# First query group of batches 1 to 3: one unsplit fp32 score product, three tiles in one PSUM bank, and another judge of the planned order

## The chip, the cores and the metric

The program runs on one core of one Trainium2 chip. The metric is the device time of one execution in microseconds (us). A core has the engines PE (TensorE, matrix products), ACT (ScalarE), DVE (VectorE), POOL (GpSimd) and SP (SyncE, which here only issues transfers). Products land in PSUM, which has eight banks of 512 fp32 columns on each of 128 partitions.

## The reference: what is computed

Block-causal attention over 4 batches, 8 heads, 576 positions and head size 64, and behind it two feed-forward layers over the 2304 x 512 result:

```python
scores = q @ k.T / sqrt(64)               # masked: 64-wide key blocks up to the query's own
x = softmax(scores) @ v                   # -> 2304 x 512
h = x @ w_in                              # 512 x 2048
y = softplus(h) @ w_out
xn = y / rms(y) * rms_g
out = (silu(xn @ w_gate) * (xn @ w_val)) @ moe2_w_out
```

All of it is held to fp32 accuracy, so most products are written as three products of split operands.

## The kernel before

**Operands and products.** TensorE takes most operands as `F32R`. An fp32 operand is split into a high part (a rounded copy) and a low part (the difference), and a product is three matmuls: high by high, high by low, low by high (`PASSES`). The alternative is one matmul on fp32 operands as they are ("unsplit"), which the trace records as two weight loads and two matmul records, where a split product has three of each.

**Attention.** A unit `u` is (batch b, query group g, head pair p). There are 48: 4 batches, 3 groups of 192 queries, 4 head pairs. A unit has three tiles (`ib` 0 to 2), each of 128 rows (64 queries of two heads) against `n = 64*(3g+ib+1)` keys: 64, 128 and 192 keys in group 0. `s_tile` (from L594) makes a tile's scores with its product (L617 to L619), then takes the row maximum on DVE (L627) and calls `s_exp` (exponential on ACT from the same PSUM bank, L661), `s_norm` (L669, L670) and `s_split` (L681 to L686), after which a transposing transfer (`pt<-pst`, L693) turns the probabilities for the product with V in `pv`. Every score tile has a PSUM bank of its own. `R_a` gives three banks to scores and to the outputs of `pv` once batch 0 is done.

**Batch 0** (`whole(u)`, units 0 to 11) already uses unsplit fp32 scores, straight from the loaded q and k, and scales the maximum with a small operation (L639). **Batches 1 to 3** (36 units) split q and k first: `prep_q` (L533) copies q into the high part (L327 on ACT or L329 on POOL), takes the difference (L337 on DVE or L338 on POOL) into `qbd`, and then issues the load of q for unit u+2 into the freed slot of `qf` (two slots). `prep_k` (L541) makes `khl` from the loaded k (L547 ACT, L552 DVE). The loaded k and v share a ring `R_raw` of three buffers.

**Layer 1** runs beside attention: `g1` (L817, `b<-x,w`) makes h for 384 rows and 128 features, ACT and DVE make softplus into a ring buffer `t` (L833 to L836) and split it into `g` (L327, L337), and `g2` (`b<-g,w`) multiplies by the second matrix. `R_t` is the ring of `t` with four buffers; the squares of `evac_b` (L889) and the gating of layer 2 (L931 to L935) use it too. Layer 2 is `g34` and `g5`, from about 600 us to the end.

**Order.** No engine's order is written out by hand. Every operation is handed to `Plan` with an engine, an assumed duration and a due time (`key`). `Plan.schedule` lays them out in time; `Plan.emit` (L268) repeats this, each time mixing the due times with the latest possible starts of the last layout, and emits all operations by the starts of the best layout. Each engine, and SP's queue too, then runs its list strictly in that order. `schedule` also models TensorE's clock, with a fixed offset of 0.7 us between the plan's time and the clock's windows.

Of the kernel before, what the change touches and what calls it, by code (L numbers as in the profile page):

```python
# [68 lines left out]
class Plan:  # L69
# [72 lines left out]

        return (e == "POOL" and not self.ops[i][6]) or (e == "DVE" and i in self.shared)

    def schedule(self, key):

        n = len(self.ops)
        eng, took = [o[0] for o in self.ops], [o[1] for o in self.ops]
# [40 lines left out]
        for _ in range(n):  # L189
# [24 lines left out]
                port_free = t + dur  # L214
            start[i] = t
            if e == "PE":
                rest, share, dur, z = dur, self.cols[i] / dur, 0.0, t + 0.7
# [53 lines left out]
    def emit(self):  # L271
        n = len(self.ops)
        self.edges()
        key = [o[2] for o in self.ops]
        best = None
        for r in range(12):
            try:
                end, start, ends, bank, choice, eng, took = self.schedule(key)
            except TypeError:
                break  # L280
            if best is None or end < best[0]:
                best = (end, start, bank, choice, key)
# [61 lines left out]
def kernel(  # L344
# [63 lines left out]
    R_x = Ring(com, 2, [128, KD, 2, BLK], F32R, "x")  # L408
    R_y = Ring(com, 1, [128, KD, BLK], FP32, "y")
    R_g = Ring(com, 3, [128, 2, BLK], F32R, "g")  # L410
    R_t = Ring(com, 4, [128, BLK], FP32, "t")
    R_wraw = Ring(com, 2, [128, CW], U64, "wraw")
    R_wa = Ring(com, 2, [128, CW], FP32, "wa")
    R_wA = Ring(wp, NA, [128, 2, 2, CW], F32R, "w")
# [6 lines left out]
    def mm(o, l, r, start, stop):  # L421
        nc.tensor.matmul(o, lhsT=l, rhs=r, start=start, stop=stop)  # L422
# [54 lines left out]
    qf = [kp.tile([128, NG, 128], FP32, name=f"qf{i}") for i in range(NQF)]  # L477
    qbd = [kp.tile([128, 2, NG, 128], F32R, name=f"qbd{i}") for i in range(2)]
    R_raw = Ring(ap_, 3, [128, KT * 128], FP32, "raw")
    R_am = Ring(ap_, 2, [128, 3], FP32, "am")  # L480
    R_P = Ring(ap_, 3, [128, KT * 128], FP32, "P")
    R_nm = Ring(ap_, 2, [128, 16], FP32, "nm")
# [12 lines left out]
    def whole(u):  # L495
        return u < 12

    def load_k(b, p, key):
        t = raw["k", b, p] = R_raw.new()
        att_ops.append(load(key, lambda: t()[:, 0:S], kT[b, p], writes=[t], nbytes=294912))  # L500

    k_y = R_y.new()
    k_raw = [R_raw.new() for p in range(2, NP)]
# [26 lines left out]
        att_ops.append(load(key, lambda: t().rearrange("p (a b) -> p a b", a=KT), vP[b, p], writes=[t], nbytes=327680))  # L530

    def prep_q(u, key):
        if whole(u):  # L533
            return
        t, d = qf[u % 2].rearrange("p i c -> p (i c)"), qbd[u % 2].rearrange("p l i c -> p l (i c)")
        hi, lo = (lambda: d[:, 0]), (lambda: d[:, 1])
        rd = [("qf", u % 2)]
        aop2(copies(nc, 384, hi, lambda: t, ("ACT", "POOL")), key, rd, [("qbd", u % 2, 0)])
        aop2(differences(nc, 384, lo, lambda: t, lambda: hi().bitcast(FP32), ("DVE", "POOL")), key, rd + [("qbd", u % 2, 0)], [("qbd", u % 2, 1)])
        if u + 2 < len(units):  # L540
            load_q(u + 2, key)  # L541
# [41 lines left out]
    def ring_a(u):  # L583
        return R_a0 if u * NG < len(units) * NG // NB else R_a
# [7 lines left out]
    part = {}  # L592

    def s_tile(u, ib, key, after):  # L594
        b, g, p = units[u]
# [10 lines left out]
        if whole(u):  # L606
            kt, k = k_cell(p), lambda: k0(p)
            (qc, qt), kr = q_slot(u), [kt]
            qr = [qc]
        bank = []  # L610
        for c0, cn in chunks:
            sp = ring_a(u).new()
            bank.append(sp)

            def qk(sp=sp, c0=c0, cn=cn):
                if whole(u):
                    mm(sp()[:, :cn], qt()[:, ib, :], k()[:, c0:c0 + cn], True, True)  # L617
                    return
                for m, (a, c) in enumerate(PASSES):  # L619
                    mm(sp()[:, :cn], d[:, a, ib, :], khl[p][:, c, c0:c0 + cn], m == 0, m == 2)  # L620

            if c0 == 0:
                qk_op.append(len(plan.ops))
            aop("PE", max(0.213, 0.006 + cn * 1.667e-3) if whole(u) else 3 * t_mm(cn), key, qk, qr + kr, [sp], after=after, cols=t_mm16((4 if whole(u) else 3) * cn))
        for c, (sp, (c0, cn)) in enumerate(zip(bank, chunks)):
            col = ib + c
            aop("DVE", t_dve(cn), key, lambda sp=sp, col=col, cn=cn: nc.vector.tensor_reduce(nm()[:, col:col + 1], sp()[:, :cn], axis=AX.X, op=ALU.max, negate=True), [sp], [(nm, ib)])  # L627
# [3 lines left out]
        if whole(u):  # L631
            if 0:
                if ib < NG - 1:
                    return
                todo, i0, i1 = done, 0, NG
            else:
                todo, i0, i1 = [done[-1]], ib, ib + 1
# [14 lines left out]

    def s_exp(u, ib, n, bank, chunks, key):
        nm, done = part[u]
        P = part[u, ib] = R_P.new()
        scale = 0.125 if whole(u) else 1.0
        if n % 128:
            aop("POOL", 0.09, key, lambda: nc.gpsimd.memset(P()[:, n:n + 64], 0.0), [], [(P, "pad")])
        for c, (sp, (c0, cn)) in enumerate(zip(bank, chunks)):
            col = 4 + ib + c  # L660
            aop("ACT", 0.24 + cn * 0.836e-3, key, lambda sp=sp, col=col, c0=c0, cn=cn: nc.scalar.activation(P()[:, c0:c0 + cn], sp()[:, :cn], ACTF.Exp, scale=scale, bias=nm()[:, ib:ib + 1], accum_out=nm()[:, col:col + 1]), [sp, (nm, ib)], [P, (nm, "s", ib)])  # L661
# [127 lines left out]
    def attention(t0, t1, when, after):  # L789
        nt = len(tiles)  # L790
        for t in range(t0, t1):
            if t < nt:
# [6 lines left out]
                    load_v(b + 1, p, when(t) - 5)  # L799
                if ib == NG - 1 and b + 1 < B and g == NG - 1 and True:  # L800
                    load_k(b + 1, p, when(t) - 5)
                if ib == NG - 1 and whole(u):
                    if u + 4 < 12 + 2:
                        load_q(u + 4, when(t) - 5)
# [366 lines left out]
```

## Time and profile before

| | before |
|---|---|
| median of 3 runs (lowest to highest) | 1040.03 us (1039.77 to 1041.62) |
| the profiled execution: its own time | 1040.05 us |
| its span, first to last instruction | 1038.3 us |
| PE busy | 1009.9 us (97%) |
| DVE, ACT, POOL busy | 667.8, 580.1, 214.0 us |
| granted TensorE clock, mean | 0.998 |

The profiled execution is thus one of the median's kind, and 1.75 us lie outside of its span. The page's rows count an engine as busy while an instruction runs; a wait row names an instruction that started late, the instruction or transfer that released it, and for how long the engine sat idle before.

### The profile page before, as it was taken

How to read it: one execution, taken by the hardware profiler on the slowest of the kernel's cores; microseconds unless marked ns; L12 is line 12 of the kernel's file. 1: busy time of each engine (PE TensorE's matmuls, PEld its weight loads, DVE VectorE, ACT ScalarE, POOL GpSimd, SP SyncE). 2: the span in 40 equal slices, each digit the busy share in tenths (PEclk: the TensorE clock that was granted, in tenths of full speed). 3: DMA queues.
4: the chain of work that ended last, by engine and by line, in shares of the span. 5: the costliest groups of instructions: out<-in, count | busy, mean ns of one | idle time of the engine just before them, and what ended most of it. 6: DMA issues, size and time to landing. Idle time of an engine off the chain costs nothing.

```text
span 1038.3 us, 16885 instructions
## 1 busy us (share of the span) xinstructions
PE 1009.9 (97%) x6136; PEld 941.9 (91%) x6136; DVE 667.8 (64%) x1592; ACT 580.1 (56%) x1352; POOL 214.0 (21%) x289
## 2 busy tenths in 40 slices
PE   5999899999999999999999999999999999999998
PEld 4677898999989999999999999999999999999997
DVE  6899999887888677777888899422422423222322
ACT  6999798777778678877878664211211212111111
POOL 3543433331233023223324342000000000000000
PEclk9999999999999999999999999999999999999999
DMA  7454787958556635456444634200100100000000
GB/s 263 133 194 150 191 196 167 252 116 201 130 132 117 111 102 183 164 209 212 162 158 159 199 102 142 69 1 1 62 1 1 62 1 1 31 1 1 31 1 31
DMA packets 111635, 115.19 MB, mean 111 GB/s; under 512 B 84544, under 2 KB 92352, under 8 KB 110528
## 3 DMA queue, kind: packets, MB, share of 16 engines
q1 hardware_dynamic: 110976, 107.83, 36.8%
q0 software_dynamic: 576, 6.29, 1.6%
q8 instruction: 48, 0.79, 0.3%
q14 instruction: 35, 0.29, 0.1%
HBM read 72.03 MB, written 21.63 MB: 90 GB/s over the span
## 4 chain that ended last, share of the span: by engine, by line
PE 73%; DVE 9%; ACT 8%; DMA 7%; issue 2%; POOL 1%; SPq 0%; POOLq 0%; ACTq 0%; DVEq 0%
PE b L422 73%; DMA pt<-pst 4%; DMA wraw<-in_w_dram 2%; ACT P L661 1%; POOL wa L461 1%; ACT wa L448 1%; DVE wa L456 1%; DVE g L337 1%; ACT w L327 1%; DVE nm L627 1%; DVE wa L458 1%; DVE pst L686 1%; DVE t L836 1%; ACT t L834 1%; ACT P L705 1%
## 5 line engine op out<-in xcount | busy, mean ns | idle before, releaser
L422 PE MATMUL b<-x,w 128*128 128x384 f32 x2880 | 543.6, 338 | 2.0 <-DVE nm L669 0.8
L422 PEld LDWEIGHTS b<-x,w 128*128 128x128 f32 x2880 | 503.8, 188 | 13.8 <-issue 1.3
L422 PE MATMUL b<-g,w 128*128 128x384 f32 x1152 | 229.8, 339 | 2.2 <-DVE g L337 1.9
L422 PEld LDWEIGHTS b<-g,w 128*128 128x128 f32 x1152 | 199.4, 188 | 6.5 <-DVE g L337 3.6
L422 PE MATMUL b<-w,g 128*128 128x512 f32 x648 | 160.4, 392 | 0.0
L932 DVE TENSOR_TENSOR t<-b,t 128x384 f32<-128x384 f32 x72 | 40.0, 556 | 165.3 <-ACT t L931 165.1
L422 PEld LDWEIGHTS b<-w,g 128*128 128x128 f32 x648 | 120.6, 188 | 21.8
L461 POOL TENSOR_TENSOR wa<-wa,wraw 128x512 int32<-128x512 int32 x68 | 95.2, 1401 | 204.0 <-DVE wa L456 119.1
L931 ACT ACTIVATE t<-b 128x384 f32<-128x384 f32 x72 | 35.2, 490 | 171.8 <-PE b L422 171.8
L934 ACT CAST g<-t 128x384 fp32r<-128x384 f32 x72 | 36.8, 513 | 136.4 <-DVE t L933 136.4
L661 ACT ACTIVATE P<-b,nm 128x288 f32<-128x288 f32 (+8 forms) x160 | 80.1, 502 | 16.3 <-DVE nm L639 4.5
L627 DVE TENSOR_REDUCE nm<-b 128x1 f32<-128x288 f32 (+8 forms) x160 | 70.7, 447 | 18.7 <-PE b L422 17.6
L933 DVE TENSOR_TENSOR t<-b,t 128x384 f32<-128x384 f32 x72 | 39.9, 556 | 61.5 <-PE b L422 61.5
L686 DVE SCALAR_TENSOR_TENSOR pst<-P,nm,pst 128x128 f16<-128x128 f32 (+4 forms) x108 | 68.3, 638 | 9.1 <-ACT pst L683 6.7
L422 PE MATMUL b<-khl,qbd 128*128 128x448 f32 (+7 forms) x360 | 68.9, 312 | 1.0 <-ACT pt L722 1.0
L337 DVE TENSOR_TENSOR g<-t,g 128x384 fp32r<-128x384 f32 x96 | 60.5, 632 | 11.4 <-ACT g L327 10.9
L836 DVE SCALAR_TENSOR_TENSOR t<-b,t 128x384 f32<-128x384 f32 x96 | 52.6, 551 | 21.4 <-ACT t L835 21.0
L935 DVE TENSOR_TENSOR g<-t,g 128x384 fp32r<-128x384 f32 x72 | 42.9, 597 | 35.4 <-ACT g L934 35.4
L422 PEld LDWEIGHTS b<-khl,qbd 128*128 128x128 f32 x360 | 57.1, 188 | 3.9 <-ACT pt L722 1.2
L327 ACT CAST g<-t 128x384 fp32r<-128x384 f32 x96 | 49.2, 516 | 19.9 <-DVE t L836 16.8
L448 ACT ACTIVATE wa<-wraw 128x512 f32<-128x512 f32 x68 | 46.1, 678 | 20.9 <-DMA wraw<-in_w2gv_dram 10.7
L833 ACT ACTIVATE t<-b 128x384 f32<-128x384 f32 x96 | 46.5, 493 | 19.1 <-PE b L422 19.0
(91 smaller groups left out, 1055.7 us busy)
## 6 DMA issues: line engine op xcount, KB each, us to landing
wraw<-in_w_dram SPq DMA_DIRECT2D x32, 512.0 KB, 3.6
wraw<-in_w2gv_dram SPq DMA_DIRECT2D x24, 512.0 KB, 3.6
yd<-y SPq DMA_DIRECT2D x12, 768.0 KB, 3.7
y<-yd SPq DMA_DIRECT2D x12, 768.0 KB, 4.5
qf<-in_qP_dram SPq DMA_DIRECT2D x42, 192.0 KB, 2.8
xd<-x SPq DMA_DIRECT2D x4, 1536.0 KB, 7.1
x<-xd POOLq DMA_DIRECT2D x4, 1536.0 KB, 7.4
wraw<-in_w2o_dram SPq DMA_DIRECT2D x12, 512.0 KB, 4.4
```

The source lines that it names most:

```text
L327: "ACT": ("ACT", t_act(n), lambda: nc.scalar.copy(dst(), src())),
L337: "DVE": ("DVE", t_dve(n), lambda: nc.vector.tensor_tensor(dst(), a(), b(), ALU.subtract)),
L422: nc.tensor.matmul(o, lhsT=l, rhs=r, start=start, stop=stop)
L448: op("ACT", t_act(CW), prio, lambda a=a, hv=halves: nc.scalar.activation(a(), hv()[1].bitcast(FP32), ACTF.Abs), [raw], [a])
L461: op("POOL", t_pool2(CW), prio, lambda a=a, hv=halves: nc.gpsimd.tensor_tensor(a().bitcast(I32), a().bitcast(I32), hv()[0].bitcast(I32), A ...
L627: aop("DVE", t_dve(cn), key, lambda sp=sp, col=col, cn=cn: nc.vector.tensor_reduce(nm()[:, col:col + 1], sp()[:, :cn], axis=AX.X, op=ALU.m ...
L661: aop("ACT", 0.24 + cn * 0.836e-3, key, lambda sp=sp, col=col, c0=c0, cn=cn: nc.scalar.activation(P()[:, c0:c0 + cn], sp()[:, :cn], ACTF.E ...
L686: aop("DVE", t_dve(c, True), key, lambda: nc.vector.scalar_tensor_tensor(lo(), pc(), r(), hi(), ALU.mult, ALU.subtract), [P, (P, "pad"), ( ...
L833: op("ACT", t_act(BLK, False), key - 5, lambda: nc.scalar.activation(e(), h()[:, :BLK], ACTF.Abs), [h], [e])
L836: op("DVE", t_dve(BLK), key - 5, lambda: nc.vector.scalar_tensor_tensor(e(), h()[:, :BLK], 0.0, e(), ALU.max, ALU.add), [h, e], [e])
L932: op("DVE", t_dve(BLK), key + 2, lambda: nc.vector.tensor_tensor(u(), ga()[:, :BLK], u(), ALU.mult), [ga, u], [u])
L935: op("DVE", t_dve(BLK), key + 4, lambda: nc.vector.tensor_tensor(g()[:, 1], u(), g()[:, 0].bitcast(FP32), ALU.subtract), [u, (g, 0)], [(g, ...
```

## The change

1. `unsplit(u)` is `whole(u)` or group 0. The 12 units of group 0 in batches 1 to 3 now make each score tile as one fp32 product of the loaded q and the first 192 columns of the loaded k. These columns get a buffer and a transfer of their own (`R_kg`, two buffers, one 96 KB load per unit, issued behind the load of k). `prep_q` does nothing for these units.
2. Their maximum is scaled by the small operation that batch 0 uses, on DVE or POOL, and the exponential takes the scale 0.125.
3. The three tiles of a group-0 unit go to columns 0, 64 and 192 of one bank; in the plan, each third of the bank is a cell of its own.
4. The load of q for unit u+2 behind a group-0 unit of batches 1 to 3 is issued behind that unit's third tile, not behind its `prep_q`.
5. `R_t` has three buffers instead of four.
6. `emit` makes up to 60 layouts instead of 12 and judges each by its mean end over three clock offsets (0.7, 1.8, 2.9 us). A layout that can't be completed no longer ends the search; its due times are averaged with the best ones.

```diff
+    PHASES = (0.7, 1.8, 2.9)
+    def schedule(self, key, phase=PHASES[0]):
...
-        for r in range(12):
+        for r in range(60):
...
+                mean = (end + sum(self.schedule(key, p)[0] for p in self.PHASES[1:])) / len(self.PHASES)
...
+            if best is None or mean < best[0]:
+                best = (mean, start, bank, choice, key)
...
-    R_t = Ring(com, 4, [128, BLK], FP32, "t")
+    R_t = Ring(com, 3, [128, BLK], FP32, "t")
...
+    R_kg = Ring(ap_, 2, [128, GQ], FP32, "kg")
...
+    def unsplit(u):
+        return whole(u) or units[u][1] == 0
...
+        k = kg[b, p] = R_kg.new()
+        att_ops.append(load(key, k, kT[b, p][:, 0:GQ], writes=[k], nbytes=98304))
...
     def prep_q(u, key):
-        if whole(u):
+        if unsplit(u):
             return
...
+        elif unsplit(u):
+            (qc, qt), k = q_slot(u), kg[b, p]
+            qr, kr = [qc], [k]
         bank = []
+        o0 = (0, 64, 192)[ib] if g == 0 else 0
         for c0, cn in chunks:
-            sp = ring_a(u).new()
+            if g == 0 and ib:
+                sp = packed[u]
+            else:
+                sp = packed[u] = ring_a(u).new()
...
+                if unsplit(u):
+                    mm(sp()[:, o0:o0 + cn], qt()[:, ib, :], k()[:, c0:c0 + cn], True, True)
                     return
...
+                if ib == NG - 1 and unsplit(u) and not whole(u) and u + 2 < len(units):
+                    load_q(u + 2, when(t) - 4)
```

(The packing of item 3 goes by `g == 0`, so the four group-0 units of batch 0 are packed too.)

## Rows read from the trace of the kernel before

**Rows 1.** The page: span, and busy time, share and instructions of each engine.

```profile
span 1038.3 us, 16885 instructions
PE 1009.9 (97%) x6136; PEld 941.9 (91%) x6136; DVE 667.8 (64%) x1592; ACT 580.1 (56%) x1352; POOL 214.0 (21%) x289
```

**Rows 2.** Busy time by stretch: stretch, length, PE, PEld, DVE, ACT, POOL, clock, DMA.

```profile
60.00:140.00 80.00, 73.93 (x512) 64.37 (x511) 75.67 (x227) 71.57 (x181) 34.42 (x51) 1.00 0.61 170
140.00:360.00 220.00, 216.40 (x1711) 202.24 (x1710) 188.48 (x571) 174.41 (x461) 60.13 (x118) 1.00 0.69 155
360.00:600.00 240.00, 238.88 (x1379) 235.02 (x1379) 189.41 (x331) 184.53 (x372) 78.27 (x58) 1.00 0.51 172
```

**Rows 3.** What PE waited for, all of the span: total us, times, longest.

```profile
PE b L422 <- DMA qf<-in_qP_dram: 4.4, 1, 4.4
PE b L422 <- ACT pt L722: 3.0, 4, 1.4
```

**Rows 4.** Chain that ended last, its longest piece: start, us, what.

```profile
582.01 451.67 PE b L422 x2377
```

**Rows 5.** PE in order of time, around a split group-0 unit of batch 3.

```profile
275.82 0.51 PE L422 MATMUL b<-x,w 128*128 128x384 f32 x2
276.17 1.14 PE L422 MATMUL b<-khl,qbd 128*128 128x64 f32 x9
277.15 1.07 PE L422 MATMUL b<-g,w 128*128 128x384 f32 x5
```

**Rows 6.** PE in order of time, unsplit group-0 tiles of batch 0.

```profile
10.05 0.38 PE L422 MATMUL b<-y,pst 128*128 128x64 f32 x2
...
22.50 1.04 PE L422 MATMUL b<-raw,qf 128*128 128x64 f32 x6
...
34.01 0.49 PE L422 MATMUL b<-raw,pst 128*128 128x192 f32 x2
34.20 1.35 PE L422 MATMUL b<-x,w 128*128 128x384 f32 x6
35.39 0.49 PE L716 MATMUL b<-ones,P 128*128 128x128 f32 x3
```

**Rows 7.** PE in order of time, a group-0 tile of batch 1 that waited.

```profile
95.02 0.58 PE L422 MATMUL b<-khl,qbd 128*128 128x192 f32 x3 [1.01 <-ACT pt L722]
```

**Rows 8.** Instructions on `qbd`: duration ns min/median/max, first and last start.

```profile
L338 POOL TENSOR_TENSOR qbd<-qf,qbd x22: 999/1024/1608, 59.8 to 334.9; 128x384 fp32r<-128x384 f32 x22
L327 ACT CAST qbd<-qf x22: 495/510/655, 64.0 to 334.3; 128x384 fp32r<-128x384 f32 x22
L337 DVE TENSOR_TENSOR qbd<-qf,qbd x14: 541/547/860, 99.0 to 313.4; 128x384 fp32r<-128x384 f32 x14
```

**Rows 9.** The scaling of the maximum in batch 0, on DVE, same columns.

```profile
L639 DVE TENSOR_SCALAR nm<-nm x24: 133/143/155, 5.3 to 90.8; 128x1 f32<-128x1 f32 x24
```

**Rows 10.** PE and DVE in order of time: units 0 and 13, scores and maxima.

```profile
4.38 3.75 PE L422 MATMUL b<-y,qf 128*128 128x64 f32 x10 [4.38 <-DMA qf<-in_qP_dram]
5.07 0.23 DVE L627 TENSOR_REDUCE nm<-b 128x1 f32<-128x64 f32 x1 [5.07 <-PE b L422]
...
107.66 0.28 DVE L627 TENSOR_REDUCE nm<-b 128x1 f32<-128x128 f32 x1
107.73 0.47 PE L422 MATMUL b<-khl,qbd 128*128 128x192 f32 x3
```

**Rows 11.** Loads of q, us to landing; PE in order of time, units 14 and 16.

```profile
DMA to landing us min/median/max: 2.3/2.8/6.7
...
114.75 0.38 PE L422 MATMUL b<-khl,qbd 128*128 128x192 f32 x2
...
119.12 0.51 PE L422 MATMUL b<-khl,qbd 128*128 128x256 f32 x3
```

**Rows 12.** ACT and DVE in order of time: a fourth `t` begins.

```profile
255.64 0.49 ACT L833 ACTIVATE t<-b 128x384 f32<-128x384 f32 x1
255.54 0.55 DVE L337 TENSOR_TENSOR g<-t,g 128x384 fp32r<-128x384 f32 x1
```

More of the change, by code (lines that the diff above doesn't have):

```diff
@@ L143, in on_port @@
         return (e == "POOL" and not self.ops[i][6]) or (e == "DVE" and i in self.shared)
-    def schedule(self, key):
+    PHASES = (0.7, 1.8, 2.9)
+    def schedule(self, key, phase=PHASES[0]):
         n = len(self.ops)
@@ L216, in schedule @@
             if e == "PE":
-                rest, share, dur, z = dur, self.cols[i] / dur, 0.0, t + 0.7
+                rest, share, dur, z = dur, self.cols[i] / dur, 0.0, t + phase
                 while rest > 1e-9:
@@ L279, in emit @@
             except TypeError:
-                break
-            if best is None or end < best[0]:
-                best = (end, start, bank, choice, key)
+                if best is None:
+                    raise
+                key = [(x + y) / 2 for x, y in zip(key, best[4])]
+                continue
+            try:
+                mean = (end + sum(self.schedule(key, p)[0] for p in self.PHASES[1:])) / len(self.PHASES)
+            except TypeError:
+                mean = INF
+            if best is None or mean < best[0]:
+                best = (mean, start, bank, choice, key)
             late = self.latest(start, ends, eng, took)
@@ L496, in whole @@
         return u < 12
+    def unsplit(u):
+        return whole(u) or units[u][1] == 0
+    kg = {}
     def load_k(b, p, key):
@@ L590, in small @@
         aop2([e[k] for k in kind], key, reads, writes, False)
-    part = {}
+    part, packed = {}, {}
     def s_tile(u, ib, key, after):
@@ L609, in s_tile @@
             qr = [qc]
+        elif unsplit(u):
+            (qc, qt), k = q_slot(u), kg[b, p]
+            qr, kr = [qc], [k]
         bank = []
+        o0 = (0, 64, 192)[ib] if g == 0 else 0
         for c0, cn in chunks:
-            sp = ring_a(u).new()
+            if g == 0 and ib:
+                sp = packed[u]
+            else:
+                sp = packed[u] = ring_a(u).new()
             bank.append(sp)
             def qk(sp=sp, c0=c0, cn=cn):
-                if whole(u):
-                    mm(sp()[:, :cn], qt()[:, ib, :], k()[:, c0:c0 + cn], True, True)
+                if unsplit(u):
+                    mm(sp()[:, o0:o0 + cn], qt()[:, ib, :], k()[:, c0:c0 + cn], True, True)
                     return
                 for m, (a, c) in enumerate(PASSES):
-                    mm(sp()[:, :cn], d[:, a, ib, :], khl[p][:, c, c0:c0 + cn], m == 0, m == 2)
+                    mm(sp()[:, o0:o0 + cn], d[:, a, ib, :], khl[p][:, c, c0:c0 + cn], m == 0, m == 2)
             if c0 == 0:
                 qk_op.append(len(plan.ops))
-            aop("PE", max(0.213, 0.006 + cn * 1.667e-3) if whole(u) else 3 * t_mm(cn), key, qk, qr + kr, [sp], after=after, cols=t_mm16((4 if whole(u) else 3) * cn))
+            aop("PE", max(0.213 if whole(u) else 0.11, 0.006 + cn * 1.667e-3) if unsplit(u) else 3 * t_mm(cn), key, qk, qr + kr, [(sp, ib)], after=after, cols=t_mm16((4 if unsplit(u) else 3) * cn))
         for c, (sp, (c0, cn)) in enumerate(zip(bank, chunks)):
             col = ib + c
-            aop("DVE", t_dve(cn), key, lambda sp=sp, col=col, cn=cn: nc.vector.tensor_reduce(nm()[:, col:col + 1], sp()[:, :cn], axis=AX.X, op=ALU.max, negate=True), [sp], [(nm, ib)])
+            aop("DVE", t_dve(cn), key, lambda sp=sp, col=col, cn=cn: nc.vector.tensor_reduce(nm()[:, col:col + 1], sp()[:, o0:o0 + cn], axis=AX.X, op=ALU.max, negate=True), [(sp, ib)], [(nm, ib)])
         if len(chunks) == 2:
@@ L630, in s_tile @@
         done.append((ib, n, bank, chunks, key))
[L631 to L637, printed above, removed]
+        if unsplit(u):
+            todo, i0, i1 = [done[-1]], ib, ib + 1
             cells = [(nm, i) for i in range(i0, i1)]
@@ L654, in s_exp @@
         nm, done = part[u]
+        o0 = (0, 64, 192)[ib] if units[u][1] == 0 else 0
         P = part[u, ib] = R_P.new()
-        scale = 0.125 if whole(u) else 1.0
+        scale = 0.125 if unsplit(u) else 1.0
         if n % 128:
@@ L660, in s_exp @@
             col = 4 + ib + c
-            aop("ACT", 0.24 + cn * 0.836e-3, key, lambda sp=sp, col=col, c0=c0, cn=cn: nc.scalar.activation(P()[:, c0:c0 + cn], sp()[:, :cn], ACTF.Exp, scale=scale, bias=nm()[:, ib:ib + 1], accum_out=nm()[:, col:col + 1]), [sp, (nm, ib)], [P, (nm, "s", ib)])
+            aop("ACT", 0.24 + cn * 0.836e-3, key, lambda sp=sp, col=col, c0=c0, cn=cn: nc.scalar.activation(P()[:, c0:c0 + cn], sp()[:, o0:o0 + cn], ACTF.Exp, scale=scale, bias=nm()[:, ib:ib + 1], accum_out=nm()[:, col:col + 1]), [(sp, ib), (nm, ib)], [P, (nm, "s", ib)])
         if len(chunks) == 2:
```

## The prediction

> **What bounds the kernel now.** First the page's busy shares: PE is busy in 1009.9 of 1038.3 us [rows 1], so about 28 us of the span are not PE work, 4.4 of them the first load [rows 3]. Then busy time by stretch, to see where the rest lies: PE lacks 6.1 of 80 us from 60 to 140 us, 3.6 of 220 up to 360, 1.1 of 240 up to 600 [rows 2], together 10.8; another 8 or 9 lie in the first 60 us. In the first of these stretches DVE (75.7 of 80) and ACT (71.6) are as full as PE: there attention is limited by them. From 140 us on PE sets the pace, and from 582 us the chain that ended last is one piece of 451.67 us on PE [rows 4]. So what is taken off PE's list between 140 and 360 us comes off the end one for one, as long as no new wait replaces it; what is taken off DVE or ACT counts only up to 140 us; the clock is at its full level throughout (1.00 in each stretch), so it has nothing to give back.
>
> **The change part by part.** All sums are made against the profiled execution, 1040.05 us (a span of 1038.3 and 1.75 around it), which is 0.02 above the median.
>
> *PE.* A split group-0 unit takes 0.98 us of PE, from its first start at 276.17 to the next product's at 277.15 [rows 5]. That is nine matmuls at about 0.11 us, and the 64-column ones are no cheaper than the 192-column ones: 64, 128 and 192 columns at 2.4 GHz would be 0.03, 0.05 and 0.08 us, so each is held by its own weight load. An unsplit tile has two loads instead of three. Its price from batch 0: a 64-column tile 0.38 us, less the 0.16 by which an end overlaps the next start (276.17 + 1.14 - 277.15 [rows 5]), is 0.22 [rows 6]; a 192-column tile followed by six 384-column matmuls takes 35.39 - 34.01 = 1.38 us, less six times 0.175 (two of them from 275.82 to 276.17 [rows 5]), is 0.33; a 128-column tile lies between, and I take 0.22, since four passes of 128 columns at 2.4 GHz are 0.21. Sum 0.77. The one unit of batch 0 whose three tiles ran in one piece gives 1.04 - 0.16 = 0.88 [rows 6], its first load not hidden. The gain is 0.21 per unit, at worst 0.10: times 12, **-2.5 us** (bounds -1.2 and -2.8). Eight of the twelve units lie behind 140 us, where nothing hides it; of the four before, 0.8 us, a part may turn into idle time, which the bounds take in.
>
> The Trainium skill ("TensorE: Matmul & The Clock Gate", section "Back-to-back issue gap") gives about 81 ns for each pair of a weight load and a 128-column matmul in a sustained stream. By it a split unit would take 0.73 us, an unsplit one about 0.65 by streaming, and the term would be an estimated -1 us; no row here shows a pair below 0.11, so the trace disagrees.
>
> *A wait for a bank.* The third tile of unit 12 waited 1.01 us [rows 7]; its score bank would now be that of its first two tiles. But this is the stretch where DVE and ACT are full. 0 to -1.0; I take half, **-0.5**.
>
> *The shared bank.* In the plan the thirds of a bank are free of each other. If the program keeps engines apart by whole banks, a score product can't run while DVE or ACT reads an earlier third. Of the 24 second and third tiles of batches 1 to 3, seven readings of an earlier tile (maximum or exponential) were running when a tile's product started, as at 107.73, in the midst of the maximum at 107.66 [rows 10]; their remainders add up to 0.7 us. Unit 0 has the same at the very start: its first maximum begins at 5.07 while PE still runs scores [rows 10]; the packing takes batch 0 in too, and there the maximum must wait for one or two products, 0.5 to 1.2 us. I take **+0.7** and **+0.5**; bounds 0 and, together, 2.5 (below nothing only through the banks set free, which the line before has).
>
> *Splitting and scaling.* By their start times, 12 of the 36 preparations of q are of group 0: 5 copies on ACT at 0.51, 3 differences on DVE at 0.55, the other 7 copies and 9 differences on POOL (1.02 each for a difference, up to 1.6) [rows 8]. DVE loses 1.6 us, ACT 2.6, POOL about 15. Scaling adds 36 times 0.143 us if all goes to DVE [rows 9]. In batch 1, where DVE is the limit, that is 12 x 0.143 - 0.55 = +1.2 us at most; ACT's relief and POOL's free time (a third of the scalings of batch 0 went there) speak against it. **+0.3**, bounds -0.5 and +1.2. Behind 140 us PE covers it.
>
> *Queues.* Twelve loads of 96 KB more go through SP, one small issue each; the third of a batch must wait for the first unit's products (two buffers), and the transposing transfers and weight loads queue behind it on SP. Loads of q behind a group-0 unit leave only after its third tile. From unit 14's last product at about 115 us to unit 16's first at 119.12 [rows 11] there are 4.0 us; a load takes 2.8 (up to 6.7), and copy and difference 0.51 + 0.55 to 1.02. This just fits or misses by some us, and then the planned order puts other products first. 0, bounds 0 and +2.
>
> *`t` ring.* With three buffers, one of 96 starts of `t` in layer 1 would have come too early: at 255.64, by 0.45 us, the difference running until 256.09 [rows 12]. Squares of `evac_b` likewise by up to 2 us, but off PE's path. 0.
>
> *The order.* Sixty layouts judged at three offsets find a shorter plan than twelve at one; how much of that is true on the chip no row says. What it can touch is the 19 us in which PE idles up to 600 us without the first load. I take a twentieth, **-1.0**; a new order can as well lose, so -4 and +3.
>
> Sum: -2.5 - 0.5 + 0.7 + 0.5 + 0.3 - 1.0 = -2.5, so **1037.5 us**.
>
> **The rivals.**
> *The bank couples PE to DVE and ACT (slower).* Where the new order sets a unit's second or third product behind the maximum or exponential of the tile before, PE, which runs in order, waits for engines that lag by some us (in unit 13 the first maximum came 3 us behind its product). Without the bank's two terms the sum is -3.7. With unit 0's 0.5, 0.13 us for each of the 24 later tiles eats it up, and from 0.22 on the kernel is slower by 0.2%. At 0.23: 0.5 + 5.5 - 3.7 = +2.3, **1042.3**. For it: the plan knows nothing of it. Against: in 17 of 24 cases nothing overlaps in the order before. The Trainium skill ("PSUM — Partial Sum Buffer", section "PSUM bank collisions raise a hardware error") says just this: two engines on one bank collide even at disjoint columns, so accesses must be guarded by bank, not by address. No run here shows it yet; it is why the rival has a chance of its own.
> *The new order pays.* It takes a fifth of the 19 us: -4 instead of -1, **1034.5**. For it: batch 1 idles most, and 15 us of POOL and a bank or two per unit come free there.
> *The gain is made and eaten elsewhere.* PE's list is 2.5 shorter, but late loads of q (+2) or a fuller DVE (+1.2) and an order no better give it back: **1040**.
>
> **How the numbers follow.** This kernel's measurement can tell about 0.2% from no change, 2.1 us; 1037.97 is the border. Forecast (1036 to 1039.2): 0.45, of it 0.27 faster, 0.18 same. Order pays: 0.20, faster. Eaten: 0.20, 0.18 same and 0.02 slower. Bank: 0.15, 0.12 slower, 0.03 same. So faster 0.47, same 0.39, slower 0.14. The range that leaves out 2 in 10 is 1034.0 to 1042.0; it takes in the bounds of the order's term and most of the bank's.
>
> **What would show it.** Group-0 units with six matmul records and about 0.77 us of PE; PE busy lower by about 2 us and hence its idle time unchanged; no wait as at 95.02. For the bank rival: waits of PE for L627 or L661 in front of group-0 scores, and the first exponential later than 5.52 us. For the third: waits of PE for `qf`, `kg` or L337 at the first units of group 1. The prediction is wrong if PE's idle time up to 600 us changes by more than 3 us either way: then the order, not the product, decided.

## The result, and the profile after

| | before | after |
|---|---|---|
| median of 7 runs (lowest to highest) | 1040.55 us (1039.19 to 1041.62) | 1045.85 us (1043.55 to 1050.10) |
| ratio of the runs, 95% interval | | 1.0055 [1.0037, 1.0072] |
| the profiled execution: time, span | 1040.05, 1038.3 us | 1043.55, 1041.8 us |

The kernel became 5.3 us slower; 1037.5 was forecast, and the range ended at 1042. The profiled execution of after is its fastest run, so its trace shows only 3.5 of the 5.3 us; its mean granted clock is 0.995, and the other six runs had 0.988 to 0.993.

The page of after, span and busy time, answers to [rows 1]:

```profile
span 1041.8 us, 16886 instructions
PE 1011.1 (97%) x6100; PEld 939.8 (90%) x6100; DVE 672.9 (65%) x1608; ACT 567.9 (55%) x1330; POOL 214.4 (21%) x307
```

Busy time by stretch, columns as in [rows 2]; first a row of before that [rows 2] leaves out, then after:

```profile
0.00:60.00 60.00, 47.08 (x263) 34.52 (x264) 47.29 (x170) 49.81 (x143) 25.89 (x53) 0.97 0.64 215
```

```profile
0.00:60.00 60.00, 46.82 (x251) 32.15 (x252) 46.79 (x168) 48.14 (x137) 24.34 (x46) 0.94 0.62 199
60.00:140.00 80.00, 71.73 (x487) 62.20 (x485) 73.57 (x226) 69.89 (x178) 33.56 (x54) 0.98 0.63 185
140.00:360.00 220.00, 214.99 (x1668) 200.25 (x1665) 188.46 (x578) 166.58 (x450) 62.59 (x140) 1.00 0.72 158
360.00:600.00 240.00, 240.00 (x1413) 237.02 (x1412) 192.82 (x334) 179.19 (x365) 74.87 (x56) 1.00 0.49 168
```

PE has 36 instructions fewer than before and is yet busy 1.2 us longer: the clock is lower in the first two stretches (0.94 and 0.98, where before has 0.97 and 1.00). Idle is 30.7 us instead of 28.4. Between 60 and 140 us PE lacks 8.3 us, where it lacked 6.1.

What PE waited for in after (total us, times, longest), to be held against [rows 3]:

```profile
PE b L431 <- DVE x L773: 4.7, 1, 4.7
PE b L431 <- DMA qf<-in_qP_dram: 4.4, 1, 4.4
PE b L736 <- ACT P L725: 3.2, 2, 2.0
PE b L431 <- DMA pt<-pst: 2.7, 2, 1.6
PE b L431 <- DVE nm L651: 2.5, 4, 1.3
```

The 4.4 is the first load, as before. New are one wait of 4.7 us for an `x` (L773) and four for a row maximum (L651).

Engines in order of time at the start of after, four rows picked out (start, duration, engine, line, tiles; in brackets the idle time before and its releaser), to be held against unit 0 in [rows 10]:

```profile
4.38 1.20 PE L431 MATMUL b<-y,qf 128*128 128x64 f32 x4 [4.38 <-DMA qf<-in_qP_dram]
5.61 0.22 DVE L651 TENSOR_REDUCE nm<-b 128x1 f32<-128x64 f32 x1 [5.61 <-PE b L431]
5.89 2.93 PE L431 MATMUL b<-y,qf 128*128 128x192 f32 x6 [0.32 <-DVE nm L651]
7.26 0.31 ACT L681 ACTIVATE P<-b,nm 128x64 f32<-128x64 f32 x1 [5.24 <-DVE nm L651]
```

The first maximum waits for the second product (5.61, before 5.07), the third product waits for that maximum, and the first exponential begins at 7.26 instead of 5.52. So in the running program the thirds of a bank are not free of each other as they are in the plan. These are waits that the program itself makes, for one engine's access to the bank to end before the next begins; what the chip would do without them no run shows.

PE in order of time near 100 us in after:

```profile
100.14 0.93 PE L431 MATMUL b<-kg,qf 128*128 128x64 f32 x6
100.90 0.39 PE L431 MATMUL b<-ones,am 128*128 128x128 f32 x2
...
106.47 3.91 PE L431 MATMUL b<-x,w 128*128 128x384 f32 x12 [4.67 <-DVE x L773]
110.32 1.78 PE L431 MATMUL b<-pt,pst 128*64 128x192 f32 x20
```

An unsplit unit takes 0.76 us (100.14 to 100.90), as forecast. Soon behind it lies the longest pause, and behind that half clock, as two rows by stretch of after show:

```profile
101.80:106.50 4.70, 0.04 (x2) 0.03 (x1) 4.70 (x18) 2.83 (x8) 1.91 (x6) 1.00 0.81 211
106.50:110.20 3.70, 3.70 (x12) 3.42 (x12) 2.77 (x10) 2.87 (x6) 1.86 (x2) 0.54 0.77 211
```

PE did next to nothing for 4.7 us while the granted clock was at the 2.4 GHz level (1.00), and then worked at 1.2 GHz for nearly all of the next 3.7.

### The profile page after: what moved, and what is told of

It is laid out like the page before. It is cut to its first block, busy times and chain, and to the rows that moved or that the text cites. A ratio compares the mean times of both kernels' runs of the same rounds, so it can differ in the third digit from the quotient of the medians.

```text
span 1041.8 us, 16886 instructions
## 1 busy us (share of the span) xinstructions
PE 1011.1 (97%) x6100; PEld 939.8 (90%) x6100; DVE 672.9 (65%) x1608; ACT 567.9 (55%) x1330; POOL 214.4 (21%) x307
## 4 chain that ended last, share of the span: by engine, by line
PE 82%; DVE 8%; DMA 5%; ACT 3%; issue 2%; SPq 1%; POOL 0%; ACTq 0%; DVEq 0%; POOLq 0%
PE b L431 81%; DMA pt<-pst 2%; DMA wraw<-in_w_dram 1%; DVE pst L706 1%; DVE nm L651 1%; DVE w L346 1%; DVE wa L465 1%; PE b L736 1%; ACT P L681 1%; DVE wa L467 0%; DMA qf<-in_qP_dram 0%; DVE g L957 0%; DVE x L937 0%; DVE t L955 0%; SPq L441 0%
## 5 line engine op out<-in xcount | busy, mean ns | idle before, releaser
L651 DVE TENSOR_REDUCE nm<-b 128x1 f32<-128x288 f32 (+8 forms) x160 | 69.8, 450 | 20.1 <-PE b L431 18.5
L706 DVE SCALAR_TENSOR_TENSOR pst<-P,nm,pst 128x384 f16<-128x384 f32 (+4 forms) x108 | 68.7, 649 | 7.7 <-ACT pst L703 4.0
L346 DVE TENSOR_TENSOR g<-t,g 128x384 fp32r<-128x384 f32 x96 | 60.9, 637 | 10.0 <-ACT g L336 9.4
L957 DVE TENSOR_TENSOR g<-t,g 128x384 fp32r<-128x384 f32 x72 | 40.0, 557 | 32.5 <-ACT g L956 32.5
L431 PE MATMUL b<-khl,qbd 128*128 128x448 f32 (+5 forms) x252 | 52.2, 328 | 0.9 <-DVE y L879 0.8
L857 ACT ACTIVATE t<-t 128x384 f32<-128x384 f32 x96 | 50.2, 526 | 1.2
```

The costliest lines, as they stand in the source:

```text
L346: "DVE": ("DVE", t_dve(n), lambda: nc.vector.tensor_tensor(dst(), a(), b(), ALU.subtract)),
L706: aop("DVE", t_dve(c, True), key, lambda: nc.vector.scalar_tensor_tensor(lo(), pc(), r(), hi(), ALU.mult, ALU.subtract), [P, (P, "pad"), ( ...
L857: op("ACT", t_act(BLK), key - 5, lambda: nc.scalar.activation(e(), e(), ACTF.Ln, bias=1.0), [e], [e])
```

## The experiments

"In the old order" and "in the new order" mean that the layout is that of before or of after, instruction by instruction, and only what is named differs. The other kernels lay themselves out. The planned end is what the kernel computes for its layout when it is built, at the single clock offset of 0.7 us. Ratios are to the runs of before on the same chip. Where an expectation speaks of the score tiles of units 0, 1 and 2, it counts the group-0 units of batch 0 alone (0, 2 and 4 among all units).

| run | median us | ratio [95%] | planned end | median less planned |
|---|---|---|---|---|
| before | 1040.55 | 1 | 1021.1 | 19.4 |
| after | 1045.85 | 1.0055 [1.0037, 1.0072] | 1019.8 | 26.0 |
| one_product_only | 1040.20 | 0.9995 [0.9987, 1.0004] | old order | |
| prod_in_old_order | 1055.31 | 1.0150 [1.0134, 1.0165] | old order | |
| pack_unit0_in_old_order | 1040.66 | 1.0006 [0.9995, 1.0017] | old order | |
| new_judge_old_operations | 1045.78 | 1.0048 [1.0035, 1.0061] | 1026.1 | 19.7 |
| old_judge_new_operations | 1040.83 | 1.0003 [0.9994, 1.0011] | 1018.5 | 22.3 |
| other_layout_new_operations | 1045.71 | 1.0054 [1.0041, 1.0068] | 1020.8 | 24.9 |
| old_judge_own_banks | 1043.93 | 1.0034 [1.0022, 1.0047] | 1019.55 | 24.4 |
| old_judge_late_q_planned | 1046.50 | 1.0057 [1.0045, 1.0070] | 1018.44 | 28.1 |
| early_x_in_new_order | 1046.65 | 1.0073 [1.0060, 1.0086] | new order | |
| early_x_of_units_9_10 | 1046.85 | 1.0058 [1.0039, 1.0077] | new order | |
| filled_gaps_in_new_order | 1047.12 | 1.0062 [1.0049, 1.0074] | new order | |
| no_late_q_in_new_order | 1043.99 | 1.0035 [1.0022, 1.0047] | new order | |
| unpack_batch0_in_new_order | 1044.63 | 1.0042 [1.0028, 1.0055] | new order | |
| new_order_own_banks | 1045.84 | 1.0046 [1.0033, 1.0059] | new order | |
| new_order_no_late_q_own_banks | 1040.77 | 1.0006 [0.9995, 1.0016] | new order | |
| old_judge_no_late_q | 1040.81 | 1.0006 [0.9998, 1.0015] | order of old_judge_new_operations | |
| old_judge_own_banks_unit0 | 1041.98 | 1.0016 [1.0005, 1.0026] | the same | |
| filled_gaps_old_judge | 1041.62 | 1.0011 [1.0003, 1.0020] | the same | |

### Does the unsplit product gain anything?

```diff
+                if g == 0:
+                    mm(sp()[:, :cn], d[:, 0, ib, :].bitcast(FP32), khl[p][:, 0, c0:c0 + cn].bitcast(FP32), True, True)
+                    return
```

> The kernel before, its order, banks, copies, differences and loads untouched; only TensorE's three products of each group-0 tile of batches 1 to 3 become one unsplit fp32 product of the two high parts (the low parts of q and k are left out of these scores). By the theory that the unsplit product gains what the prediction said and only the later load of q ate it in the run prod_in_old_order: 2.1 to 2.9 us faster than before, about 1038.2. By the theory that a product saved in a fixed order only turns into idle time: within 0.7 us of before.

The page of one_product_only:

```profile
span 1038.4 us, 16813 instructions
PE 1007.7 (97%) x6100; PEld 938.3 (90%) x6100; DVE 667.2 (64%) x1592; ACT 580.1 (56%) x1352; POOL 214.4 (21%) x289
```

This kernel leaves out the low parts of q and k in these scores. PE works 2.2 us less than before, and the span is the same to 0.1 us: the whole gain lies as idle time on PE. In the stretch of batch 1, from 90 to 160 us, PE waited in before for

```profile
PE b L422 <- DVE g L337: 1.2, 1, 1.2
PE b L422 <- ACT pt L722: 1.0, 1, 1.0
...
PE b L422 <- DMA pt<-pst: 0.5, 1, 0.5
PE b L422 <- ACT P L661: 0.3, 1, 0.3
```

and in one_product_only for

```profile
PE b L422 <- DMA pt<-pst: 1.8, 2, 1.3
PE b L422 <- ACT pt L725: 1.2, 1, 1.2
PE b L422 <- DVE g L337: 1.2, 1, 1.2
...
PE b L422 <- ACT P L664: 0.6, 1, 0.6
```

PE waits longer for the probabilities and their transposing transfers. That this is the gain itself, turned into waits, is likely but not shown: 2.1 of the 2.3 us of additional idle time lie between 60 and 140 us, with only 4 of the 12 units, and the same instructions on DVE and ACT start 0.6 to 2.3 us later than in before between 115 and 290 us, which PE's lighter list does not explain. What the times show is that almost nothing comes off the end: the interval leaves at most 1.4 us of gain.

### What does the later load of q cost, if the order knows nothing of it?

An unsplit product again, but of the loaded q; the splitting of q is gone, and the load leaves later.

```diff
-            load_q(u + 2, key)
+            later[u] = lambda: nc.sync.dma_start(out=tq(), in_=qP[b2, g2_, p2])   # issued behind the unit's third product
```

> The kernel before with its own order of all operations, each score tile in its own bank; only the product of the 12 group-0 units of batches 1 to 3 is one unsplit fp32 product of the loaded q, their splitting of q is gone, and the load of q for the unit after next leaves behind the unit's third product. The keys are the rounded high part of k alone (its low part is left out), so that no further load and no scaling are needed. By the theory that the unsplit product gains what the prediction said: -2.1 to -2.9 us against before, about 1037.8, with about 0.77 us of PE for such a unit instead of 0.98. By the theory that the gain is lost anywhere (late q, or idle time in its place): -1 to +1 us, with PE waiting for qf or idle longer up to 360 us.

It was 15 us slower than before. Waits of prod_in_old_order between 190 and 215 us, one row each of POOL, DVE and PE:

```profile
POOL qbd L362 <- DMA qf<-in_qP_dram: 10.4, 1, 10.4
DVE qbd L370 <- POOL qbd L362: 6.5, 1, 6.5
PE b L455 <- DVE t L922: 6.0, 1, 6.0
```

One late load stops POOL's copy, DVE's difference stands behind it in DVE's list, and layer 1's softplus stands behind that: PE waits 6 us for work that has nothing to do with q. The same instruction on DVE and ACT starts 3.7 us later than in before at 125 us, and 13.7 us later at 220 us. So in an order that does not plan for it the load's place is worth far more than the product; neither of the two theories had foreseen a loss of this size.

### Does the shared bank delay at the start go through?

```diff
+                sx, o0 = shared[u], (0, 64, 192)[ib]      # the first three group-0 units of batch 0
```

> The kernel before with its own order and its split products; only the three score tiles of units 0, 1 and 2 (group 0 of batch 0) share one bank each, at columns 0, 64 and 192. By the theory that the shared bank couples the engines and that the start of the kernel goes straight into its end: the first exponential starts 1 to 1.8 us later than 5.52 us, and the kernel is 1 to 1.8 us slower. By the theory that the delay is taken up later, since PE idles several us up to 140 us: the first exponential is as late, and the time within 0.5 us of before.

The first DVE and ACT work is 1.2 to 1.6 us late, and at 10 us 0.17: the pauses of the old order take it up. The second theory holds, in this order.

### Is it the search or the operations?

```diff
-        for r in range(60):
+        for r in range(12):
...
-                mean = (end + sum(self.schedule(key, p)[0] for p in self.PHASES[1:])) / len(self.PHASES)
+                mean = end
```

> The changed kernel with the old search: 12 layouts, judged at the single clock offset of 0.7 us. It takes another layout (planned end 1018.5 us, where the changed kernel's own is 1019.8 at that offset). By the theory that the new operations cost the time in any order (bank, late q, scaling): the same 23.7 us between plan and chip, hence about 1042.5 to 1045. By the theory that the picked order alone lost, and the old search picks better: 18.9 us between plan and chip as before, hence about 1037.5, at most 1040.

The reverse, the new search with the operations of before:

> The kernel before, all its operations, with the new search alone (60 layouts, judged by their mean end over three clock offsets). It takes another layout than before: mean planned end 1023.1 us where the old one's is 1024.7, but 1026.1 against 1021.1 at the single offset of 0.7 us. By the theory that the search, not the operations, made the loss: slower than before, by 2 to 5 us (1042.5 to 1045.5). By the theory that the operations made it and the mean over offsets judges rightly: 1 to 2 us faster than before, about 1039.

And the sixth layout of the new search (`if r == 5:`):

> The changed kernel with another layout of its own search: the sixth, whose mean planned end (1021.2 us) is 1.1 later than that of the one it takes (1020.06) and 0.8 later than the old judge's (1020.4). It sizes what a layout is worth on the chip beside its planned end. Its longest planned pauses of PE behind 30 us are 2.0 us, where the one taken has 5.7. By the clock theory: clock 0.995 or more and 1040 to 1043. By the theory that the plan ranks layouts rightly: 1 us slower than the changed kernel, 1046 to 1048.

With the old search the changed operations run as fast as before (1040.83, between the ranges of both theories); with the new one the old operations run 5.0 us slower. So the layout that the new search takes makes nearly the whole loss, with either set of operations. Both searches go through the same layouts in the same order as far as the old one goes: of the changed operations the new search takes the eighth and the old one the third, of the old operations the sixth and the fifth. So the 48 further layouts changed nothing; the mean over three offsets, which is the judge, took the slower layout.

In both pairs the single offset ranks the layouts rightly and the mean wrongly: for the old operations planned 1021.1 and 1026.1 (mean 1024.7 and 1023.1), measured 1040.5 and 1045.8; for the changed ones 1018.5 and 1019.8 (mean 1020.4 and 1020.06), measured 1040.83 and 1045.85. That the single offset is the better judge does not follow. Among the changed operations the planned end says little at either judge: five layouts planned between 1018.4 and 1020.8 (two of them with one part changed, below) ran between 1040.8 and 1046.5, and two of these that the single offset took were slow. Of seven layouts measured in all, two ran within 0.5 us of 1040.5; whether the new judge is worse or only had the commoner luck stays open. The sixth layout has a clock of 0.997 in its profile, about that of before, and is as slow as after, so a high clock alone doesn't make a good layout. My bet on 1040 to 1043 for it was wrong.

### What is wrong with the new order? The pause at 102 us

```diff
+        for i, j in self.moves:              # the differences for x of units 9 and 10
+            start[i] = start[j] + 0.35       # right behind their copies on ACT
```

> The changed kernel with its own order but for one operation: the DVE difference for x of the last unit of batch 0 (it started at 106.08 us, ten us behind its ACT copy, and PE's next matmul waited 4.67 us for it) goes right behind that copy. By the theory that the order makes the loss, through this gap and the half clock behind it: the 4.67 us gap shrinks to under 1.5 us, the clock stays full near 107 to 110 us, and 3.5 to 6.5 us come back: 1039.5 to 1042.5. By the bank theory, in which DVE and ACT are held up all over batch 1 and the gap only shows it: PE idles elsewhere up to 140 us instead, and at most 1.5 us come back: 1044.3 to 1046.

This first try moved the difference of unit 11, for which nobody waits; the pause stayed at 4.65 us. The second moved the right ones:

> The changed kernel in its own order, but the DVE differences for x of units 9 and 10 of batch 0 (at 106.08 and 108.01 us there) go right behind their ACT copies (93.32 and 95.78 us), which frees the two PSUM banks that PE waits for in its 4.67 us gap. The run early_x_in_new_order had moved the difference of unit 11, which nobody waits for so long. By the theory that the gap of the new order is the loss: the gap under 1.5 us, no half clock at 107 to 110 us, and 3.5 to 6.5 us back against 1045.85: 1039.5 to 1042.5. By the theory that DVE and ACT set the pace of batch 1 and the gap is only their reserve: PE idles as long in other places up to 140 us, and less than 1.5 us come back: 1044.3 to 1046.

PE in order of time in early_x_of_units_9_10:

```profile
103.90 2.25 PE L435 MATMUL b<-x,w 128*128 128x384 f32 x12
110.30 3.21 PE L435 MATMUL b<-pt,pst 128*64 128x192 f32 x20 [4.15 <-ACT P L685]
```

The twelve matmuls run without a pause, and PE then waits 4.15 us for an exponential instead: the product with V begins at 110.30, in after at 110.32. DVE's and ACT's instructions stand 2.1 us behind those of after at 90 us and 2.5 at 120: nothing was won in between. (Those 2.1 us arose before the edit begins, in the first 60 us, where this profile's clock is 0.89 and that of after 0.94.) The half clock has moved with the pause: the twenty matmuls behind it take 3.21 us, where after has 1.78. The median of 1046.85 us lies above both ranges, so taking the pause away here brought nothing back: it is a reserve of PE, and the loss lies elsewhere.

### The half clock

39 extra matmuls keep PE busy ahead of the three stretches of half clock (from 18.06, 41.95 and about 106.5 us in the profile of after).

```diff
+                for _ in range(count):
+                    self.mm(tile[:, c:c + 128], self.ones, self.ones, own, own)
```

> The changed kernel, its order and all its work, with 39 extra matmuls of 128 columns (ones by ones, into PSUM columns that nothing reads, about 0.2 us each) put into PE's gaps ahead of the three stretches of half clock, at 15 to 18, 36 to 42 and 102 to 106 us of the changed kernel's trace. They do nothing but keep PE busy. By the clock theory (the new layout's longer pauses of PE bring the half clock, and each such stretch of 3.4 us costs up to 1.7 us): the mean granted clock back at 0.996 or more, fewer stretches of half clock up to 110 us, and 2.5 to 5 us less than the changed kernel's 1045.85: 1041 to 1043.5. By the theory that DVE, ACT and late loads make the loss and the clock only follows: clock higher but the time within 1 us of 1045.85. If the extra matmuls only get in the way: slower than 1046.

Busy time by stretch of filled_gaps_in_new_order:

```profile
0.00:60.00 60.00, 49.83 (x300) 36.96 (x300) 47.72 (x170) 48.88 (x138) 25.33 (x48) 1.00 0.61 203
60.00:140.00 80.00, 73.63 (x490) 65.07 (x489) 70.97 (x222) 66.76 (x171) 32.11 (x49) 0.96 0.65 177
```

The clock is full for the first 60 us (after: 0.94), and the work at 90 us is 0.6 us earlier than in after; between 60 and 140 us the clock is 0.96, lower than in after (0.98), so there the half clock has only moved. None of the gain reaches the end: 1047.12 us is no faster than after and, by the letter of the expectation, the third case, in which the extra matmuls get in the way. This profile alone can't tell the clock from the extra work. With the old search:

> The kernel of the run old_judge_new_operations (1040.83 us) with 19 such extra matmuls in PE's gaps between 13 and 25 us of its trace, ahead of its only stretch of half clock (25.4 to 28.8 us, after 2.27 us of idle PE). By the clock theory: no half clock at 25 us and 0.5 to 1.7 us less, 1039.1 to 1040.3. By the other theory: within 0.5 us.

It was not faster either (1041.62), and in its profile, too, the clock is 1.00 up to 60 us and 0.96 from 60 to 140. What decides is the runs whose mean clock was 1.000: 1047.25 and 1047.37 us for filled_gaps_in_new_order, and, without any extra matmul, 1044.23 us for old_judge_late_q_planned (below) and 1039.57 us for old_judge_new_operations. So a full clock leaves the differences between layouts as they are. Within one kernel the time does go with the clock: after took 1043.55 us at 0.995 and 1050.10 at 0.988.

### Late loads and shared banks in the new order

```diff
+        if u >= 14 and unsplit(u - 2):       # no_late_q: 12 loads of q left out
+            return
...
+            if g == 0 and ib and whole(u):   # own banks, where one is free
+                own[u, ib] = Extra(banks, sp)
```

> The changed kernel in its own order; the 12 loads of q that it issues behind a group-0 unit's third tile are left out (those units of group 1 work on the q of another unit), so that nothing waits for them. By the theory that the late load of q is a main part of the loss: the wait of 1.18 us of ACT for qf at 123 us goes, and 1.3 to 4 us come back: 1042 to 1044.5. By the theory that the plan has made room for it: within 0.7 us of 1045.85.

> The changed kernel with its own order; only the second and third score tiles of units 0 and 1 get banks of their own again (for the other units of batch 0 none is free in this order). By the bank theory: the first exponential back at 5.5 instead of 7.26 us, and 1 to 1.8 us less than the changed kernel's median 1045.85, about 1044.4. By the order theory, which puts the loss on the long gap of PE near 100 us: within 0.5 us of 1045.85, since that gap ends with DVE's work and takes the start's delay up.

unpack_batch0_in_new_order took 1044.63 us, but in it two other units of batch 0, for which no bank was free, had all three tiles in columns 0 on, one over the other; new_order_own_banks is the same edit with only the first two touched.

> The changed kernel, its order and all its work; only the second and third score tiles of units 0 and 1 have PSUM banks of their own. Against the changed kernel's 1045.85 us, leaving out the late loads of q gave -1.9, and both edits together -5.1. By the theory that the two add up: -3.2, so 1042.7. By the theory that the start's delay is taken up by later waits unless these are gone too: within 1 us of 1045.85, and the two only count together.

> The changed kernel, its order kept; the 12 late loads of q are left out as in no_late_q_in_new_order (1043.99 us), and the second and third score tiles of units 0 and 1 have banks of their own. By the theory that the shared bank at the start (first exponential 1.74 us later) goes through to the end in this order: 1.0 to 1.8 us less, 1042.2 to 1043. By the theory that PE's later pauses take it up: within 0.5 us of 1043.99.

Own banks alone gave nothing (1045.84), no late loads alone 1.9 us (its interval overlaps that of after), both together 5.1 us: the loss is gone, in a kernel that leaves out 12 loads. By the medians the two do not add up. How the start of the same DVE and ACT instructions stands to that in the profile of after (median of some twenty, us; negative is earlier):

| planned time | no late q | own banks | both | filled gaps |
|---|---|---|---|---|
| 5 us | 0.0 | -1.3 | -1.3 | 0.0 |
| 30 us | +1.5 | -0.4 | -1.3 | -0.3 |
| 90 us | +2.0 | -0.2 | -1.6 | -0.6 |
| 120 us | +1.1 | +1.1 | -3.0 | -1.0 |
| 150 us | +0.2 | +1.3 | -4.2 | +0.7 |
| 960 us | -0.5 | +2.5 | -4.3 | +2.9 |
| granted clock, 0 to 60 us | 0.89 | 0.91 | 0.97 | 1.00 |

The start's 1.3 us are mostly lost again within 30 us in the profile with the lower clock (own banks, 0.91) and kept in the other (both, 0.97), though up to there both kernels run the same instructions. In the same way the first column loses 1.5 us by 30 us and 2.0 by 90, at a clock of 0.89, before the first of the loads left out (96.8 us in after). So these losses come from the run, not from the edit. From 90 us to the end the two profiles without the late loads gain 2.5 and 2.7 us on after, and the two with them lose 2.7 and 3.5 on it. By this the late loads cost more in this order than the 1.9 us of the medians, and the start shows or not with the clock of the first 60 us; four profiles suggest this and don't prove it. In after, ACT waits between 110 and 128 us for such a load:

```profile
ACT qbd L336 <- DMA qf<-in_qP_dram: 1.2, 1, 1.2
```

Each column is one profile, and the clock differs from run to run of one kernel; the medians of the first table carry the verdict.

### The same two in the order of the old search

> The kernel of the run old_judge_new_operations (1040.83 us), its order kept; the 12 loads of q behind a group-0 unit's third tile are left out, so those units of group 1 work on another unit's q. By the theory that the late loads of q eat the gain of the product: 1.5 to 2.5 us less, 1038.3 to 1039.3, with the slip at 170 to 180 us of the plan gone. By the theory that other engines set the pace there: within 0.7 us of 1040.83.

> The kernel of the run old_judge_new_operations (1040.83 us), its order and all its work; only the second and third score tiles of unit 0 have banks of their own (no others are free in this order). By the theory that a start 1.3 us earlier goes through to the end: 1.0 to 1.6 us less, about 1039.5, faster than the kernel before. By the theory that it is taken up within the first 20 us, as in pack_unit0_in_old_order: within 0.5 us of 1040.83.

Neither helps there: the loads cost nothing (1040.81 against 1040.83), and own banks for unit 0 make it no faster (1041.98). Two more kernels were laid out by the old search, one without the packing and one told that a load of q takes 3 us (`done=3`):

> The changed operations with the old search and without the packing: every score tile has a PSUM bank of its own, as before. The layout is another one; its planned end is 1019.55 us, 1.0 later than that of old_judge_new_operations. By the theory that the shared bank costs 1.3 us at the start, or more in batches 1 to 3, which the plan doesn't know: the chip is 1.3 or more closer to the plan, so 1040.5 or below. By the theory that it costs nothing that lasts, the same 22.3 us beyond the plan: 1041.8.

> The changed operations with the old search and the packing; the plan alone is told that a load of q lands 3 us behind its issue instead of 1 (a load took 2.8 us in the trace). Planned end 1018.44 us, the same as without that to 0.1 us. By the theory that late loads of q are what lies between plan and chip beyond before's 19.4 us: 1038 to 1039.3, faster than before. By the theory that they are not: 1040.7, as old_judge_new_operations.

Both came out slower, the second by 5.7 us, at a planned end that is the same to 0.1 us and with the clock at 0.995 and more. (The first ran at 1043.93 us with a clock of 0.993 to 0.996.) No reason of mine explains that; what a new layout gets or loses is larger than what I tried to mend.

## Why the prediction was wrong, point by point

*The order, -1.0 (bounds -4 and +3).* This is the step that failed. The search alone cost +5.0 us with the old operations and, with the new ones, 5.0 against the old search; both lie outside of the bounds, and no row stood behind the upper one. I had argued from the pauses that a layout can touch, and took the planned end as a measure of a layout. It isn't one at this scale: median less planned end is 19.4 for before and 22.3 to 28.1 for the changed operations. The sign given for recognising this was a change of PE's idle time up to 600 us by over 3 us. It changed by +2.8 in the profile of after (23.7 to 26.5, by the rows by stretch from 0 to 600 us), which is the fastest run; so the sign was just missed, though what it stood for is what happened.

*PE, -2.5.* The price of a product was right: 0.76 us for a unit where 0.77 was worked out, 2.2 us less PE work in one_product_only. A second step that failed is that it "comes off the end one for one": 0.5 us came off, at most 1.4, where the bounds were 1.2 and 2.8. The share of PE behind 140 us, 216 of 220 us, said that PE is busy, not that nothing else is late next. The rival "gain made and eaten elsewhere" had this right in outline, and its 1040 is near what one_product_only measured (1040.20); but there neither late loads nor a fuller DVE, the reasons that it names, can have eaten the gain, so the agreement is in part luck.

*The shared bank, +0.7 and +0.5, bounds to 2.5.* The mechanism is as the rival told it. The first exponential comes 1.74 us later, and PE waits four times, 2.5 us in all, in front of a unit's second or third tile for the maximum of an earlier one; one of these waits is that at the start, and two are in batches 1 to 3. The Trainium skill ("PSUM — Partial Sum Buffer", section "PSUM bank collisions raise a hardware error") says that accesses must be guarded by bank, not by address. The trace shows a program that does so, with 5.61 for the first maximum where before has 5.07; a collision no run shows. Its place in the sum is another matter: packed in the old order it cost 0.2 us, within the measurement's uncertainty; own banks in the new order gave 0, and 3.2 us once the late loads were gone, part of which, in the profiles, is the clock of the start. The rival's time of 1042.3 was the nearest of the four to 1045.85, but its reason isn't shown to carry it alone.

*Queues, 0 (bounds 0 and +2).* Too small. In the new order leaving out the late loads gave 1.9 us, and 5.1 with own banks at the start in both kernels; in the old order, which doesn't plan for it, the later load cost 15 us with all that stands behind it; in the old search's order it cost nothing.

*The wait at 95.02, -0.5.* Not to be told apart; PE's idle time in this stretch grew.

*Scaling, +0.3, and the `t` ring, 0.* Not tried alone. Both are in old_judge_new_operations, which is at 1.0003. The smaller ring in the old order was not tried, since the order of before needs its fourth buffer.

*"The clock has nothing to give back."* Nearly true of before, whose mean is 0.998; but "1.00 in each stretch" was read from 60 us on, and the row of the first 60 us has 0.97. More to the point, the clock could fall further, and fell behind pauses (0.94 there in after). The runs at a full clock show that this alone is not the loss.

What is shown is that the layout taken by the new judge makes the loss. What stays open is why: layouts whose planned ends agree to 1 or 2 us run up to 6 us apart, with clocks alike. For the layout of after, the late loads together with the shared bank at the start account for the loss; the slow layout of the old operations has neither, and its reason wasn't found. No kernel of this study beat before by more than the noise.

## What to carry to other kernels

Where a program lays out its own order, any edit, even to the search alone, draws a new layout. Hold the order fixed and change one thing to learn what that thing is worth, and draw several layouts to learn what a layout is worth; here that was 5 us and more, twice the gain sought. A step taken off an engine that is 97% busy need not come off the end: read what that engine's next wait would be before putting the gain there. A load that has to wait for its buffer is dear through what is queued behind its reader on each engine.

## What was not expected of the hardware

- With three tiles in one bank the program's waits make DVE's first maximum start behind PE's next product (5.61, before 5.07), PE wait for the maximum, and the first exponential come at 7.26 us instead of 5.52.
- After 4.7 us with 0.04 us of PE work the granted clock was 0.54 over the next 3.7 us, so twelve matmuls took 3.91 us; the same twelve took 2.25 us without the pause.
- Filling such pauses with matmuls kept the clock at 1.00 for the first 60 us and gave no time (1047.12 against 1045.85 us); two runs of that kernel with a mean clock of 1.000 took 1047.25 and 1047.37 us.
